# Step 1's first convolution block: three pairs by DMA and three adds on VectorE; two lists reordered; another PSUM bank for the side products

## The chip, the cores and the metric

The kernel runs on one core of one Trainium2 chip. The metric is the time of one execution on the device in microseconds, the median of three runs; lower is better. The core has TensorE (PE, matmuls), VectorE (DVE), ScalarE (ACT), GpSimd (POOL) and SyncE (SP). POOL and SP also issue DMAs, each from a queue of its own, worked off in order.

## The reference, cut to what matters

A causal convolution over the sequence with 7 taps, whose weights are a softmax per head, feeds a two-layer feed-forward block:

```python
w = softmax(weight)                             # 8 heads x 7 taps
out[b, s, h] = sum_k w[h, k] * x_pad[b, s + k, h]  # B=8, S=4096, D=192
x = out.reshape(B * S, D)                       # 32768 tokens
h = x @ w_in                                    # 192 -> 2048
g = h * (1.0 / (1.0 + np.exp(-1.702 * h)))
return g @ w_out                                # 2048 -> 192
```

Everything is in fp32.

## The kernel before, in words

**Tiling.** The tokens are worked off in 32 steps ("big" 0 to 31); each takes 512 tokens of two halves of the batch. A step has a convolution, a first product into the hidden layer (`hidden`, called once for each of two halves `v`, or `plain` in step 0), the gelu, and a second product (`second`, or `second_first` in step 0). Both products are done by schemes in the manner of Strassen: sums of blocks of the operands, fewer products, and sums of their results. Step s + 1's convolution is computed while step s's products run, so that TensorE need not wait.

**The convolution.** A step's input has three blocks of 64 channels, c = 0, 1, 2. Block 1 is computed on DVE (`conv`, L504). For blocks 0 and 2, ACT multiplies the input by each tap into a place of its own (`tap`, L515), and the taps are then added. For step 1 they are added by DMAs that accumulate, issued on POOL (`end_taps`, L529), along a tree (`TREE`): with the places numbered 0 to 6, after tap 2 the pair 1 += 2, after tap 4 the pair 3 += 4, and after tap 6 the pair 5 += 6 and then 0 += 1, 3 += 5 and 0 += 3, the last three each waiting for what they read. For step 2 block 0 goes by the same tree and block 2 by GpSimd adds (L517).

**Sums of blocks.** `prepare` yields a step's work in order: block 1 on DVE, a wait for the taps, eight sums and differences of blocks (`SUMS_C`, L393 and L391; V1 first, for step 1 on DVE), and copies over to the other half of the partitions by DMAs on SP (`cross`, L540): V1 alone, then the four blocks below C31, and after the last sum the remaining eight, C31 to V8. `need(label)` works the list off up to a label: "conv 1" (block 1), "first 1" (V1 and its copy), "all 1" (everything).

**Step 0's second product** (`second_first`) is an order written out by hand. PE runs 42 steps of it; in each, `go` puts three matmuls of 32 output columns side by side and one matmul of a side list (`aside`, L820) into the fourth quarter of a PSUM bank (`sums[0]`, `sums[1]` or `c12`), from where ACT copies finished sums away (L822). DVE makes its operands: t1, t2 (sums of blocks of g, 128x2048 each), s1 to s4 (of w_out), and `sums_b` (L827). At the same time ACT copies and POOL's DMAs build the sums of w_out that later steps use (`add_forms`, stages 0 to 3: COPY_O by ACT, L435 and L433; SUMS_O by accumulating DMAs on POOL, L437; some read what an earlier one made). ACT changes the sign of four of these at the end (`end_forms`, L441). DVE makes 20 sums of blocks of w_in in place (`SUMS_W`, `sums_w_in`). Taps of step 2 are put between (`next_tap`); their places are rows of g.

**What sets the order.** Each engine runs its instructions in program order, and waits for what the next one needs. POOL's queue holds, in this order: the adding DMAs of step 1's taps, block 2 and then block 0; add_forms stages 0, 1 and 2; the DMAs of step 2's block 0; one GpSimd add; add_forms stage 3; further GpSimd adds. SP's queue holds step 1's three copies over, the stores of step 0's output, and the loads of x for step 3.

Step 1's first half begins with `pe(x, 5)`, that is block 0 of w_in with C11, then `pe(sums, 12)`, block 13 with V4, which is among the eight blocks copied last. In the second half the fifth product needs ACT's copy of `sums` (L646), which stands behind `end_forms` in ACT's queue.

Of the kernel before, what the change touches and what calls it, by code (L numbers as in the profile page):

```python
# [15 lines left out]
def kernel(  # L16
# [64 lines left out]
    vec, act = nc.vector, nc.scalar  # L81
# [28 lines left out]
    sums = [psum.tile([P, TOK], F32, name=f"sums{h}") for h in range(2)]  # L110
# [59 lines left out]
    def place(big, b):  # L170

        if b == V1:
            return V8 if big % 2 else C31
        return C31 if b == V8 and big % 2 else b

    def own(big):
        return conv_t[:, big % 2 * 2, :, :]
# [3 lines left out]
    NA = 21  # L181
    w_in_s = consts.tile([P, NA, UW], F32)
    SUMS_W = [
        (12, 10, "n", 11),
        (13, 12, "-", 2),
        (14, 3, "-", 12),
        (12, 1, "-", 13),
        (15, 4, "+", 13),
        (16, 3, "+", 5),
        (17, 2, "+", 5),  # L190
        (18, 0, "+", 3),
        (19, 6, "+", 8),
        (20, 19, "+", 10),
        (4, 4, "n", 16),
        (5, 2, "+", 11),
        (0, 0, "+", 2),
        (10, 7, "-", 10),
        (7, 7, "+", 19),
        (8, 8, "-", 11),
        (11, 9, "+", 11),  # L200
        (11, 11, "-", 19),
        (9, 9, "-", 3),
        (3, 3, "0", 3),
    ]

    TERMS = [
# [12 lines left out]
    def form(i):  # L219

        if i < WHOLE:
            return w_out_s[:, i // NG, i % NG * NG : (i % NG + 1) * NG, :]
        return w_form[:, i - WHOLE, :, :]
# [165 lines left out]
    def add_up(v, dst, a, op, b, eng=vec):  # L389
        if op == "+":  # L390
            eng.tensor_add(v(dst), v(a), v(b))  # L391
        elif op == "-":
            eng.tensor_sub(v(dst), v(a), v(b))  # L393
        elif op == "n":
            vec.scalar_tensor_tensor(
                out=v(dst), in0=v(a), scalar=-1.0, in1=v(b), op0=ALU.mult, op1=ALU.subtract
            )
        else:
            vec.tensor_scalar_mul(v(dst), v(a), -1.0)

    def sums_w_in(i):
        add_up(lambda j: w_in_s[:, j, :], *SUMS_W[i])

# [26 lines left out]
    def add_forms(stage):  # L430
        for dst, src, *sign in COPY_O[stage]:
            if sign:
                act.mul(form(dst), form(src), -1.0)  # L433
            else:
                act.copy(form(dst), form(src))  # L435
        for dst, src in SUMS_O[stage]:
            nc.gpsimd.dma_start(out=form(dst), in_=form(src), accum_op=ALU.add)  # L437
# [49 lines left out]
    def tap_home(big, c, k):  # L487
        if big == 1:
            return homes_1[c][k - 1]
        if big < 3:  # L490
            return (first_taps if c == 0 else taps[3])[k - 1]
        return taps[c][k - 1]

    def conv_src(big, c, k, ns=slice(0, 2)):
        return xts[big][:, c, ns, Q - PAD + k : Q - PAD + k + T]

    def conv(big, c, k, ns=slice(0, 2), times=vec.tensor_scalar_mul):
        src = conv_src(big, c, k, ns)
        dst = own(big)[:, 2 * c + ns.start : 2 * c + ns.stop, :]
        tap = cw[:, c, k : k + 1]  # L500
        if k == 0:
            times(dst, src, tap)
        else:
            vec.scalar_tensor_tensor(  # L504
                out=dst, in0=src, scalar=tap, in1=dst, op0=ALU.mult, op1=ALU.add
            )

    DMA_TAPS = (0,)
    TREE = {2: [(1, 2)], 4: [(3, 4)], 6: [(5, 6), (0, 1), (3, 5), (0, 3)]}

    def tap(big, c, k):

        dst = own(big)[:, 2 * c : 2 * c + 2, :]
        home = tap_home(big, c, k) if k else dst
        act.mul(home, conv_src(big, c, k), cw[:, c, k : k + 1])  # L515
        if k and c not in DMA_TAPS and big > 1:
            nc.gpsimd.tensor_add(dst, dst, home)  # L517
            return
        homes = [dst] + [tap_home(big, c, i) for i in range(1, K)]
        for a, b in TREE.get(k, ()):  # L520
            tree.append((homes[a], homes[b]))
        end_taps(2 if big == 2 and k == K - 1 else 0)

# [2 lines left out]
    def end_taps(left=0):  # L526
        while len(tree) > left:
            out, src = tree.pop(0)
            nc.gpsimd.dma_start(out=out, in_=src, accum_op=ALU.add)  # L529

    def sums_c(big, i):
        add_up(
            lambda j: own(big)[:, place(big, j), :],
            *SUMS_C[i],
            eng=vec if big == 1 else nc.gpsimd,
        )
# [28 lines left out]
    def cross_when(early, *what):  # L565
        if given[early] < what[0] - 1:
            waiting[early].append(what)
        else:
            cross_now(early, *what)
# [7 lines left out]
    def prepare(big):  # L577

        v1 = place(big, V1)
        def convs(*cs):  # L580
            for c in cs:
                for k in range(K):
                    yield "", 0.76 if k else 0.48, lambda c=c, k=k: conv(big, c, k)

        cost = 0.34 if big == 1 else 0.0
        yield from convs(1)
        yield f"conv {big}", 0.0, lambda: None
        yield f"done {big}", 0.0, lambda: need(f"taps {big}")
        yield "", cost, lambda: sums_c(big, 0)
        yield f"first {big}", 0.0, lambda: cross_when(True, big, v1, v1 + 1)  # L590
        yield "", 0.0, lambda: cross_when(False, big, 0, C31)
        for i in range(1, len(SUMS_C)):
            yield "", cost, lambda i=i: sums_c(big, i)
        rest = (C31, V8) if big % 2 else (C31 + 1, NB)
        yield f"all {big}", 0.0, lambda: cross_when(False, big, *rest)
# [159 lines left out]
    def chunk_cols(c):  # L755
        return slice(c * Q, (c + 1) * Q)

    def second_first(between, fetch, last_taps):
# [7 lines left out]
        def place4(t):  # L766
            return t.rearrange("p (v h e) -> p v h e", v=2, h=2)
# [3 lines left out]
        def rows4(n, pi):  # L771
            return pairs[:, :, pi // 2, n, :, pi % 2, :]
# [3 lines left out]
        b11, b12, b21, b22 = ([rows4(n, pi[j]) for pi in groups] for j in range(2) for n in range(2))  # L776
# [4 lines left out]
        t2 = [place4(flat_room[:, t4 : 2 * t4]), place4(osbs)]  # L781
# [10 lines left out]
        add, sub = vec.tensor_add, vec.tensor_sub  # L792
        js = slice(0, TOK // Q)

        c11, a, c12, c21 = (slots[i][h] for h in range(2) for i in range(2))
        side = []

        def listed(w, t, gs=(0, 1)):
            return [
                (w[i][:, v, h, :], t[i][:, v, :, h * T : (h + 1) * T])  # L800
                for i in gs for v in range(2) for h in range(2)
            ]
# [9 lines left out]
        def go(bank, steps, first=True, more=False):  # L812
            for i, (w, t) in enumerate(steps):
                for c in range(NC):
                    nc.tensor.matmul(
                        chunk(bank, c), w[:, chunk_cols(c)], t,
                        start=first and i == 0, stop=not more and i == len(steps) - 1, skip_group_check=True,
                    )
                dst, w, t, start, to = side.pop(0)
                nc.tensor.matmul(dst, w, t, start=start, stop=to is not False, skip_group_check=True)  # L820
                if to is not False:
                    act.copy(to, dst)  # L822
# [3 lines left out]
        def sums_b(i):  # L826
            sub(b12[i], b22[i], b12[i])  # L827
# [8 lines left out]

        p2, p3 = listed(a12, b21), listed(s4, b22)
        aside(
            (sums[0], sums[1], c12),
            (listed(s1, t1, (0,)), None, True), (listed(s1, t1, (1,)), p5, False), (p3[:6], q12, False),  # L840
        )
        last_taps()
# [5 lines left out]
        for i in range(2):  # L848
            sub(s2[i], s1[i], a11[i])
        add_forms(0)  # L850
        need("conv 1")
        for i in range(2):
            sub(s4[i], a12[i], s2[i])
            sub(s3[i], a11[i], a21[i])
        go(c11, p2[:6], more=True)
        add_forms(1)
        sums_b(0)
        sums_b(1)
        go(a, listed(s2, t2), first=False)
        act.copy(whole(c12), whole(a))  # L860
        go(c11, p2[6:], first=False)
        need("first 1")
        sub(t2[0], b21[0], t2[0])
        sub(t2[1], b21[1], t2[1])
        need("all 1")
        add(p1, p1, whole(c11))
        go(a, listed(s3, b12), first=False)
        add_forms(2)
# [4 lines left out]
        fetch()  # L873
        for i in range(len(SUMS_W)):
            sums_w_in(i)
# [22 lines left out]
    def chunk(t, c):  # L898
        return t[c * Q : (c + 1) * Q]
# [155 lines left out]
    def need(label):  # L1055
        for q in (todo, ready):
            while any(item[0] == label for item in q):
                q.pop(0)[2]()
# [179 lines left out]
    def fetch(big, v, slot):  # L1238

        need(f"first {big}")  # L1240
        terms(big, v, slot, 16, first=True)
# [6 lines left out]
    for big in range(1, N_BIG):  # L1248
        more = big + 1 < N_BIG
        last = hidden(big, 0, x, z, y, sums, work, lambda: fetch(big, 1, z))  # L1250
        x, z, y, sums = z, x, sums, y
# [39 lines left out]
```

## Time and profile before

| | |
|---|---|
| median of 3 runs | 2292.73 us (2292.44 to 2292.82) |
| profiled execution, its own time | 2293.8 us |
| its span (first to last instruction) | 2292.1 us |
| PE busy in the span | 2271.0 us (99%) |
| DVE, ACT, POOL busy | 1935.3, 1563.6, 844.4 us |
| granted TensorE clock, mean | 0.996 |

Times within the trace are counted from the start of the span. Of step 0's second product PE runs 55.9 to 94.1 us; step 1's first product begins behind it. A row of a timeline has the start, the duration, engine, line, operation and tiles (out<-in), how many instructions are merged in it, and in brackets the idle time of the engine before it with what ended it. Line numbers are those of the kernel before.

### The profile page before, as it was taken

What the parts mean: (1) busy time and instruction counts of PE and PEld (TensorE: products, weight loads), DVE (VectorE), ACT (ScalarE), POOL (GpSimd) and SP (SyncE); (2) the same over time, 40 slices, a digit from 0 to 9 for tenths busy, and PEclk for the clock granted to TensorE, in tenths of its full rate; (3) what the DMA queues carried; (4) which work ended last, traced back from release to release, by engine and by line L of the source; (5) the groups of instructions that cost most, each with busy time, mean ns of one, the idle gap of its engine ahead of it and who ended that gap; (6) DMA issues with size and microseconds to landing.
All of it is one profiled execution on the core that took longest, in us unless ns stands there. A gap on an engine that the chain in (4) does not pass through costs nothing.

```text
span 2292.1 us, 60960 instructions
## 1 busy us (share of the span) xinstructions
PE 2271.0 (99%) x25214; PEld 1203.4 (53%) x25214; DVE 1935.3 (84%) x2791; ACT 1563.6 (68%) x2968; POOL 844.4 (37%) x837
## 2 busy tenths in 40 slices
PE   9989999999999999999999999999999999999999
PEld 5355555555555555555555555555555555555556
DVE  8778888888888888888888888888888888888877
ACT  8647766677666677666776667776667766677754
POOL 1444433344423434334444234443334442344400
PEclk9989999999999999999999999999999999999999
DMA  9975667565665756666656656566666566564443
GB/s 204 163 143 114 115 125 141 123 130 112 125 136 121 141 111 116 125 139 125 129 113 127 134 121 140 112 114 126 139 126 128 113 127 135 122 139 86 91 98 70
DMA packets 270660, 286.56 MB, mean 125 GB/s; under 512 B 118064, under 2 KB 206128, under 8 KB 270256
## 3 DMA queue, kind: packets, MB, share of 16 engines
q0 software_dynamic: 58080, 151.48, 36.8%
q1 hardware_dynamic: 210656, 130.80, 25.3%
q8 instruction: 199, 3.26, 0.6%
q14 instruction: 77, 0.63, 0.1%
q10 hardware_dynamic: 1648, 0.39, 0.1%
HBM read 53.15 MB, written 25.17 MB: 34 GB/s over the span
## 4 chain that ended last, share of the span: by engine, by line
PE 94%; DMA 4%; DVE 1%; POOL 1%; SPq 0%; issue 0%; ACT 0%; POOLq 0%; ACTq 0%; DVEq 0%
PE slot L609 33%; PE slot L986 33%; PE sums L609 15%; PE sums L986 12%; DMA w_form<-w_form 1%; DMA g<-g 1%; DMA g<-in_moe_w_in_dram 1%; DMA conv_t<-conv_t 0%; POOL w_form L437 0%; SPq L296 0%; DMA osbs<-in_moe_w_out_dram 0%; DMA w_out_s<-w_form 0%; SPq L99 0%; ACT w_form L515 0%; POOL conv_t L529 0%
## 5 line engine op out<-in xcount | busy, mean ns | idle before, releaser
L609 PE MATMUL slot<-conv_t,w_in_s 64*128 64x512 f32 x3740 | 862.3, 593 | 9.8 <-ACT room L646 5.8
L986 PE MATMUL slot<-g,w_form 128*32 128x256 f32 x7024 | 710.3, 379 | 0.0
L609 PEld LDWEIGHTS slot<-conv_t,w_in_s 64*128 64x128 f32 x3740 | 374.8, 188 | 439.6 <-issue 354.3
L393 DVE TENSOR_TENSOR g<-g 128x1024 f32<-128x1024 f32 x372 | 451.2, 1240 | 8.1 <-ACT g L635 4.9
L986 PEld LDWEIGHTS slot<-g,w_form 128*32 128x32 f32 x7024 | 373.5, 110 | 119.7
L609 PE MATMUL sums<-conv_t,w_in_s 64*128 64x512 f32 x1660 | 407.3, 593 | 3.9 <-DMA conv_t<-conv_t 3.7
L635 ACT ACTIVATE g<-room 128x1024 f32<-128x1024 f32 x310 | 325.6, 1077 | 72.2 <-DVE room L650 72.2
L1011 ACT COPY room<-slot 32x256 f32<-32x256 f32 x434 | 159.3, 367 | 310.4 <-PE slot L986 309.3
L986 PE MATMUL sums<-g,w_form 128*32 128x256 f32 x2648 | 368.8, 379 | 0.0
L986 PE MATMUL slot<-g,w_out_s 128*32 128x256 f32 x4080 | 318.8, 380 | 0.0
L962 POOL DMA_DIRECT2D g<-g x124 | 106.4, 858 | 500.0 <-PE sums L986 166.6
L609 PEld LDWEIGHTS sums<-conv_t,w_in_s 64*128 64x128 f32 x1660 | 170.9, 188 | 191.7 <-issue 142.0
L517 POOL TENSOR_TENSOR conv_t<-conv_t,g 128x512 f32<-128x512 f32 x180 | 260.4, 1447 | 15.2 <-POOL conv_t L517 2.7
L529 POOL DMA_DIRECT2D g<-g x120 | 104.3, 884 | 428.1 <-PE sums L986 119.4
L646 ACT COPY room<-slot 128x512 f32<-128x512 f32 x434 | 231.4, 600 | 41.7 <-PE slot L609 41.7
L515 ACT ACTIVATE g<-xt,cw 128x512 f32<-128x512 f32 x360 | 248.4, 729 | 2.2
L986 PEld LDWEIGHTS slot<-g,w_out_s 128*32 128x32 f32 x4080 | 164.7, 110 | 131.7 <-ACT g L631 22.7
L631 ACT ACTIVATE g<-slot 128x512 f32<-128x512 f32 x334 | 180.7, 598 | 45.2 <-PE slot L609 25.1
L986 PEld LDWEIGHTS sums<-g,w_form 128*32 128x32 f32 x2648 | 177.9, 110 | 36.7
L504 DVE SCALAR_TENSOR_TENSOR conv_t<-xt,cw,conv_t 128x512 f32<-128x512 f32 (+1 forms) x198 | 185.6, 938 | 4.6
L393 POOL TENSOR_TENSOR conv_t<-conv_t 128x256 f32<-128x256 f32 x180 | 182.5, 1028 | 9.4
L1011 ACT COPY room<-sums 32x256 f32<-32x256 f32 x217 | 79.6, 367 | 144.7 <-PE sums L986 142.5
(203 smaller groups left out, 2901.8 us busy)
## 6 DMA issues: line engine op xcount, KB each, us to landing
g<-g POOLq DMA_DIRECT2D x124, 512.0 KB, 5.6
xin<-in_x_dram SPq DMA_DIRECT2D x240, 180.0 KB, 4.3
conv_t<-conv_t SPq DMA_DIRECT2D x180, 192.0 KB, 3.2
g<-g POOLq DMA_DIRECT2D x120, 256.0 KB, 3.9
out_dram<-osbs SPq DMA_DIRECT2D x186, 128.0 KB, 5.0
g<-room POOLq DMA_DIRECT2D x31, 512.0 KB, 5.4
conv_t<-g POOLq DMA_DIRECT2D x60, 256.0 KB, 4.6
g<-osbs POOLq DMA_DIRECT2D x30, 512.0 KB, 4.8
```

What stands on the lines that cost most here:

```text
L393: eng.tensor_sub(v(dst), v(a), v(b))
L504: vec.scalar_tensor_tensor(out=dst, in0=src, scalar=tap, in1=dst, op0=ALU.mult, op1=ALU.add)
L515: act.mul(home, conv_src(big, c, k), cw[:, c, k : k + 1])
L517: nc.gpsimd.tensor_add(dst, dst, home)
L529: nc.gpsimd.dma_start(out=out, in_=src, accum_op=ALU.add)
L609: nc.tensor.matmul(slot[h], w_in_s[halves[h], a, v * P : (v + 1) * P], src, start=first, stop=True, skip_group_check=True,)
L631: act.activation(dst[:, :, h, :], src[h].rearrange("p (o t) -> p o t", o=2), AF.Gelu_apprx_sigmoid)
L635: act.activation(dst.rearrange("p o h t -> p h o t"), src.rearrange("p h (o t) -> p h o t", o=2), AF.Gelu_apprx_sigmoid,)
L646: act.copy(bank(dst, h), bank(src, h))
L962: nc.gpsimd.dma_start(out=spot(dst), in_=spot(a), accum_op=ALU.add)
L986: nc.tensor.matmul(dst, w, t, start=first, stop=last, skip_group_check=True)
L1011: act.copy(to, d)
```

## The change

1. The taps of step 1's block 0 are added along a shorter tree, `PAIRS_1`: only the pairs 1 += 2, 3 += 4 and 5 += 6 by DMA. Three adds on DVE (128x512 each) put places 1, 3 and 5 onto place 0; they stand behind block 1 in `prepare(1)`. The three DMAs 0 += 1, 3 += 5 and 0 += 3 are gone.
2. In `second_first`, `need("first 1")` stands where `need("conv 1")` stood, so V1 and its copy come ahead of s3, s4 and `sums_b`; these are taken by halves, and `need("all 1")` comes ahead of the two t2 sums, which change places.
3. The 20 sums of w_in are in another order; each is the same sum.
4. The third bank of the side list is `c11` in place of `c12`.

```diff
     SUMS_W = [
+        (18, 0, "+", 3),
+        (0, 0, "+", 2),
         (12, 10, "n", 11),
         (13, 12, "-", 2),
...
+    PAIRS_1 = {2: [(1, 2)], 4: [(3, 4)], 6: [(5, 6)]}
...
-        for a, b in TREE.get(k, ()):
+        for a, b in (PAIRS_1 if big == 1 and c == 0 else TREE).get(k, ()):
             tree.append((homes[a], homes[b]))
...
         yield f"conv {big}", 0.0, lambda: None
+        if big == 1:
+            dst = own(1)[:, 0:2, :]
+            for k in (1, 3, 5):
+                yield "", 0.7, lambda k=k: vec.tensor_add(dst, dst, tap_home(1, 0, k))
         yield f"done {big}", 0.0, lambda: need(f"taps {big}")
...
         aside(
-            (sums[0], sums[1], c12),
+            (sums[0], sums[1], c11),
...
         add_forms(0)
-        need("conv 1")
+        need("first 1")
+        go(c11, p2[:6], more=True)
+        add_forms(1)
         for i in range(2):
             sub(s4[i], a12[i], s2[i])
             sub(s3[i], a11[i], a21[i])
-        go(c11, p2[:6], more=True)
-        add_forms(1)
-        sums_b(0)
-        sums_b(1)
+            sums_b(i)
         go(a, listed(s2, t2), first=False)
         act.copy(whole(c12), whole(a))
         go(c11, p2[6:], first=False)
-        need("first 1")
+        need("all 1")
+        sub(t2[1], b21[1], t2[1])
         sub(t2[0], b21[0], t2[0])
-        sub(t2[1], b21[1], t2[1])
-        need("all 1")
         add(p1, p1, whole(c11))
```

More of the change, by code (lines that the diff above doesn't have):

```diff
@@ L183 @@
     SUMS_W = [
+        (18, 0, "+", 3),
+        (0, 0, "+", 2),
         (12, 10, "n", 11),
         (13, 12, "-", 2),
-        (14, 3, "-", 12),
-        (12, 1, "-", 13),
-        (15, 4, "+", 13),
         (16, 3, "+", 5),
         (17, 2, "+", 5),
-        (18, 0, "+", 3),
+        (5, 2, "+", 11),
+        (14, 3, "-", 12),
+        (15, 4, "+", 13),
         (19, 6, "+", 8),
[L193 to L198, printed above, removed]
         (8, 8, "-", 11),
         (11, 9, "+", 11),
-        (11, 11, "-", 19),
         (9, 9, "-", 3),
         (3, 3, "0", 3),
+        (20, 19, "+", 10),
+        (12, 1, "-", 13),
+        (4, 4, "n", 16),
+        (10, 7, "-", 10),
+        (11, 11, "-", 19),
+        (7, 7, "+", 19),
     ]
```

## The prediction

> **What bounds the kernel now.** I read the page first, for who is busy, and then who waited for whom on PE, over the whole span.
>
> ```profile
> PE 2271.0 (99%) x25214; PEld 1203.4 (53%) x25214; DVE 1935.3 (84%) x2791; ACT 1563.6 (68%) x2968; POOL 844.4 (37%) x837
> ```
> ```profile
> PE slot L609 <- ACT room L646: 5.8, 1, 5.8
> PE slot L609 <- ACT g L631: 3.7, 1, 3.7
> PE sums L609 <- DMA conv_t<-conv_t: 3.7, 1, 3.7
> ```
>
> PE is busy nearly throughout. The reader is to see that each of these three waits happens once, and that they make 13.2 us; the other PE waits are below 1.5 us each and stand in the first 20 us. So a change in this stretch can only be worth what these waits cost. Where they stand, PE's timeline shows:
>
> ```profile
> 75.66 0.62 PE L820 MATMUL slot<-w_in_s,conv_t 128*32 128x512 f32 x1
> ...
> 76.55 0.61 PE L815 MATMUL slot<-g,conv_t 128*32 128x512 f32 x3
> ...
> 85.13 1.02 PE L820 MATMUL sums<-g,conv_t 128*32 128x512 f32 x2
> ...
> 94.14 1.13 PE L609 MATMUL slot<-conv_t,w_in_s 64*128 64x512 f32 x4
> 98.93 2.08 PE L609 MATMUL sums<-conv_t,w_in_s 64*128 64x512 f32 x4 [3.66 <-DMA conv_t<-conv_t]
> ...
> 116.03 1.90 PE L609 MATMUL sums<-conv_t,w_in_s 64*128 64x512 f32 x8
> 121.67 5.88 PE L609 MATMUL slot<-conv_t,w_in_s 64*128 64x512 f32 x16 [3.74 <-ACT g L631]
> 133.36 2.56 PE L609 MATMUL slot<-conv_t,w_in_s 64*128 64x512 f32 x4 [5.80 <-ACT room L646]
> ...
> 138.64 1.78 PE L609 MATMUL slot<-conv_t,w_in_s 64*128 64x512 f32 x4
> ```
>
> A matmul takes about 0.215 us of the row at full speed (116.03: eight in 1.90, of which 0.18 is the overlap at the end). Behind each wait they are slower. From 98.93 to the end of the 116.03 row there are 80, 17.2 us at full speed, and they took 19.0: 1.8 lost. The 16 of 121.67 took 5.88 in place of 3.4: 2.4 lost. The 16 from 133.36 to 140.42 took 7.06 in place of 3.4: 3.6 lost. Waits and slow restarts together are 13.2 + 7.8 = 21.0 us; the most that can be had.
>
> Why PE waits, ACT and POOL show, each in its own timeline:
>
> ```profile
> 92.11 1.94 ACT L515 ACTIVATE g<-xt,cw 128x512 f32<-128x512 f32 x3
> ...
> 120.08 1.06 ACT L635 ACTIVATE g<-room 128x1024 f32<-128x1024 f32 x1 [5.91 <-DVE room L650]
> ...
> 123.94 1.35 ACT L441 ACTIVATE w_form<-w_form 128x384 f32<-128x384 f32 x3
> 132.31 0.52 ACT L441 ACTIVATE w_form<-w_form 128x384 f32<-128x384 f32 x1 [7.01 <-DMA w_out_s<-w_form]
> 132.74 1.05 ACT L646 COPY room<-slot 128x512 f32<-128x512 f32 x2
> ```
> ```profile
> 62.27 2.97 POOL L529 DMA_DIRECT2D conv_t<-conv_t  x3
> ...
> 69.72 0.86 POOL L529 DMA_DIRECT2D conv_t<-conv_t  x1 [1.99 <-DMA conv_t<-conv_t]
> 74.00 0.86 POOL L529 DMA_DIRECT2D conv_t<-conv_t  x1 [3.42 <-DMA conv_t<-conv_t]
> 74.54 5.62 POOL L437 DMA_DIRECT2D w_form<-w_out_s  x6
> ...
> 80.93 5.42 POOL L437 DMA_DIRECT2D w_form<-w_out_s  x5
> ...
> 103.16 0.86 POOL L437 DMA_DIRECT2D w_form<-w_form  x1 [11.75 <-DMA w_form<-w_form]
> ...
> 105.96 3.64 POOL L529 DMA_DIRECT2D g<-g  x3
> 112.47 1.19 POOL L529 DMA_DIRECT2D conv_t<-g  x1 [2.88 <-DMA g<-g]
> 117.29 1.19 POOL L529 DMA_DIRECT2D g<-g  x1 [3.62 <-DMA g<-g]
> 123.21 1.19 POOL L529 DMA_DIRECT2D conv_t<-g  x1 [4.74 <-PE slot L609]
> ...
> 126.33 2.90 POOL L437 DMA_DIRECT2D w_out_s<-w_form  x2
> ```
>
> The **third wait** is ACT's: its copy at 132.74 stands behind the last sign change (L441), which waited for the last DMA of add_forms stage 3. That DMA is the end of POOL's queue: tap DMAs of step 1 to 74.00, forms from 74.54, a wait of 11.75 us for a form to land, step 2's tap DMAs from 105.96 in a chain of landings, then stage 3 at 126.33. The **second wait** belongs to the same queue: the gelu at 120.08 writes the rows of g that the tap DMA of 112.47 reads, so it waits for that DMA, though the profile names DVE. The **first** is the copy over of the last eight blocks. So POOL's queue is what sets the end of this stretch, and PE waits for it.
>
> **The change part by part.** *The three tree DMAs go.* POOL is done with the pairs at 62.27 + 2.97 = 65.2 and starts the forms there, not at 74.54: 9.3 us sooner. ACT's copies that the forms add to are made in the same order as before. Can the DMA engines take it? The windows say how full they are (the last two columns are their share and GB/s):
>
> ```profile
> 70.00:75.00 5.00, 5.00 (x51) 1.55 (x46) 2.87 (x2) 1.03 (x2) 1.58 (x3) 1.00 0.38 67
> 75.00:100.00 25.00, 21.34 (x172) 6.17 (x168) 21.93 (x42) 11.71 (x20) 13.09 (x15) 0.97 1.07 189
> ```
>
> They are full from 75 to 100 us and at 0.38 from 70 to 75. The full stretch holds a fixed amount of work (forms, three copies over); begun 9.3 us sooner and without idle time, it ends up to 9.3 sooner. The bounds are 0 (the copies over do not come sooner and forms only queue) and 9.3; I take 9.3, since the gap it fills is there. POOL's waiting form goes from 103.16 to 93.9, step 2's tap DMAs from 105.96 to 96.7; their last ACT taps are done at 94.05 (92.11 and 1.94).
>
> From there the chain is one of landings (median us from issue to landing in the last column; x3 are the taps of 105.96, x1 that of 117.29, w_out_s the last forms):
>
> ```profile
> conv_t<-conv_t POOLq DMA_DIRECT2D x3, 256.0 KB, 5.3
> ...
> g<-g POOLq DMA_DIRECT2D x3, 256.0 KB, 8.1
> ...
> g<-g POOLq DMA_DIRECT2D x1, 256.0 KB, 5.4
> ...
> w_out_s<-w_form POOLq DMA_DIRECT2D x2, 192.0 KB, 5.1
> ```
>
> Step 1's three pairs, of the same size and nearly alone, took 5.3 in place of 8.1, and the single DMA of 74.00 landed within 3.4 (DVE's row below) in place of 5.4. Before, the loads of x ran beside step 2's; they follow the stores, which follow DVE's last sums and hardly move, so now they fall more onto the end of the chain. This is worth between 0 and 2.8 + 2.0 = 4.8; I take 2.7, the middle. So stage 3 lands 9.3 + 2.7 = **12.0 us sooner**, and PE's third restart moves from 133.36 to 121.4.
>
> *DVE: three adds, and a new wait.* The rows that carry DVE:
>
> ```profile
> 63.48 3.11 DVE L504 SCALAR_TENSOR_TENSOR conv_t<-xt,cw,conv_t 128x512 f32<-128x512 f32 x4
> ...
> 77.37 0.42 DVE L393 TENSOR_TENSOR conv_t<-conv_t 128x256 f32<-128x256 f32 x1 [4.49 <-DMA conv_t<-conv_t]
> ...
> 84.90 0.68 DVE L866 TENSOR_TENSOR conv_t<-conv_t,slot 96x512 f32<-96x512 f32 x1
> ...
> 95.30 0.29 DVE L399 TENSOR_SCALAR w_in_s<-w_in_s 128x256 f32<-128x256 f32 x1
> ```
>
> An add of 512 columns has its nearest row at 84.90: 0.68 each, 2.0 in all. The last pair had landed at 69.72 (POOL's row), so the third add ends at 70.4 and V1 at 70.8 rather than 77.8. Queued behind this wait are s3, s4 and both `sums_b`, which PE needs from the row of 76.55 on: DVE's block between 66.6 and 72.9 (77.37 less 4.49), 6.3 us. It now runs 70.8 to 77.1, its first half done at 74, 2.5 us ahead of PE; the second half is needed half of a product later, some 3.4 us. Hidden; if the pairs landed over 2.5 us later, PE would pay the excess. The other seven sums (2.8 us, to 84.90 before) end at 80 rather than 84.9, so the eight blocks are sent 4.9 us sooner, against a wait of 3.66: the first wait goes, with 1 to 2 us to spare. The t2 sums end at 84.6, and PE takes them behind the row of 85.13 and one product more, from 86 on. All DVE work behind ends within 0.5 us of before: the new adds fill the wait of 4.49 that goes.
>
> *Order of w_in.* Block 0 is wanted first by PE (at 94.14) and was 13th of 20; all 20 were done at 95.6 (the row of 95.30). PE comes 0.9 us earlier now and does not stop behind 94.14, so the old order could cost it up to about 1.5 us with sums wanted before 95.6; with the new one, in the order in which PE wants them, nothing.
>
> *The bank.* At 75.66 a side matmul waited for ACT's copy into the same bank; the side list then ran one step late, and its last two matmuls stood alone at 85.13. With c11 that goes: 0.9 us of PE.
>
> *PE alone.* It reaches the second half at 117.93 - 0.9 - 3.7 - 1.8 + 1.0 = 112.5. The 1.0 is for new short waits (the z bank is freed by DVE, and ACT's first copy comes late); bounds 0 and 2. The gelu of 120.08 made PE wait 3.74, so at 116.3 it would have done no harm; PE being 5.4 us ahead, it now must come by 110.9. The tap DMA that it waits for lands 9.3 to 12.0 sooner, at 108 to 110.8: the second wait goes, barely. PE stands before its fifth product at 112.5 + 3.4 = 115.9 and must wait for ACT until 121.4: the third wait remains at 5.5, and with it a slow restart like the one before.
>
> **The sum.** Third restart 12.0 sooner, nothing lost or gained behind it: 2293.8 - 12.0 = 2281.8 for an execution like the profiled one, whose own time is 1.1 above the median. By the median of 2292.73 it is **2280.7**. All the PE gains (7 us) go into the last wait.
>
> The Trainium skill, "TensorE: Matmul & The Clock Gate" (What's actually happening), has the clock halve after an idle window of about 3.4 us. By that page a remaining wait well under this would save the slow restart as well; the trace agrees as far as it goes, since its three slow restarts follow waits of 3.66 and more.
>
> **The rivals.** *A: POOL's chain ends in time and all three waits go.* Then PE alone counts: 21.0 + 0.9 - 1.0 = 20.9, which is 2271.8. It needs the last sign change 17.5 us sooner (121.4 less 115.9, beside the 12.0); even the most that I found, 9.3 + 4.8 = 14.1, falls short. A shorter wait with part of the restart saved lies between, 2272 to 2276.
>
> *B: the forms only queue.* If the DMA engines, not POOL's queue, set when forms land, stage 3 lands as before, and whatever PE gains is waited for at 133.36: 2292.7, no change. For it: the share of 1.07 for 25 us. Against: the share of 0.38 just ahead, and three DMAs of 256 KB fewer.
>
> *C: slower.* POOL's 15 form issues now stand beside DVE work throughout. One issue under a busy DVE took long:
>
> ```profile
> 78.93 2.11 POOL L437 DMA_DIRECT2D w_form<-w_form  x1
> ```
>
> At 2.11 each against 0.94 (74.54: six in 5.62) POOL would lose 15 x 1.17 = 17.6 us and stage 3 come 5.6 us later than before: 2298.3. It is slower than before from 1.74 us an issue. Against it: five in 5.42 at 80.93, with DVE busy too, are 1.08 each. The Trainium skill speaks for this rival: "DMA: Bandwidth & Descriptors" (SWDGE vs HWDGE vs iDMA) says that GpSimd writes its DMAs' descriptor rings into SBUF, where VectorE can lock it out in some of its modes.
>
> **How the numbers follow.** A measurement of this kernel can tell about 0.2% (4.6 us) from no change. Forecast, 7 to 16 us sooner: 0.62. A and what lies towards it: 0.17. Between 4.6 and 7 sooner (DMA order eats part): 0.05. B, within 4.6: 0.10. C: 0.06. Faster 0.62 + 0.17 + 0.05 = 0.84, same 0.10, slower 0.06. The range leaves out B, C and the weakest gains: from A's 2271.5 to 2285.5 (7.2 sooner).
>
> **What would show it.** Right: L437 on POOL begins near 65, V1 near 70.5, no wait of PE for a copy over, L820 never alone at 85, the tap DMAs of step 2 near 97, PE's only long wait for ACT's L646 ending near 121, and it is the last sign change that holds ACT. Wrong: forms that begin at 65 but land no sooner (B), issues of 2 us (C), or a PE wait near 76 for DVE.

## The result, and the profile after

| | before | after |
|---|---|---|
| median of 6 runs each, side by side | 2292.93 us (2292.44 to 2293.97) | 2285.00 us (2283.56 to 2286.97) |
| ratio after/before, 95% interval | | 0.9965 [0.9952, 0.9978] |
| profiled execution, its own time | 2293.8 us | 2284.85 us |
| its span | 2292.1 us | 2282.9 us |

The changed kernel is 0.35% faster: 7.9 us by the medians, 8.95 between the two profiled executions. Forecast were 12.0. Lines behind L507 have other numbers now: L609 of before is L614, L646 is L651, L820 is L825, L529 is L530.

Who is busy (the page of after), and the whole span's waits of PE over 1 us (total, times, longest):

```profile
PE 2266.0 (99%) x25214; PEld 1202.3 (53%) x25214; DVE 1934.6 (85%) x2794; ACT 1563.2 (68%) x2968; POOL 847.4 (37%) x834
```
```profile
PE slot L614 <- ACT room L651: 8.6, 1, 8.6
PE sums L455 <- POOL osbs masks.py:199: 1.4, 1, 1.4
PE slot L1076 <- ACT g L1068: 1.1, 1, 1.1
```

Of the three waits in this stretch one is left, and it has grown from 5.8 to 8.6 us. PE's timeline of after shows where:

```profile
93.07 1.13 PE L614 MATMUL slot<-conv_t,w_in_s 64*128 64x512 f32 x4
94.03 1.02 PE L614 MATMUL sums<-conv_t,w_in_s 64*128 64x512 f32 x4
...
112.53 3.76 PE L614 MATMUL slot<-conv_t,w_in_s 64*128 64x512 f32 x15
124.93 2.56 PE L614 MATMUL slot<-conv_t,w_in_s 64*128 64x512 f32 x4 [8.64 <-ACT room L651]
```

At 94.03, where PE had stood 3.66 us for the last eight blocks, it goes straight on. The second half begins at 112.53 without a wait for the gelu; before, PE was ready for it at 117.93 and began at 121.67. PE stands before its fifth product at 116.29, 11.3 us ahead of before's 127.56, and goes on at 124.93, only 8.4 us ahead of 133.36. The first and second waits went. Of PE's lead of 11.3 us, 2.8 are spent in a longer third wait.

What it waits for, on ACT and POOL of after:

```profile
110.40 1.06 ACT L640 ACTIVATE g<-room 128x1024 f32<-128x1024 f32 x1 [1.78 <-DMA conv_t<-g]
...
114.26 1.35 ACT L441 ACTIVATE w_form<-w_form 128x384 f32<-128x384 f32 x3
123.88 0.52 ACT L441 ACTIVATE w_form<-w_form 128x384 f32<-128x384 f32 x1 [8.26 <-DMA w_out_s<-w_form]
124.31 1.05 ACT L651 COPY room<-slot 128x512 f32<-128x512 f32 x2
```
```profile
61.70 2.97 POOL L530 DMA_DIRECT2D conv_t<-conv_t  x3
64.09 5.88 POOL L437 DMA_DIRECT2D w_form<-w_out_s  x6
...
94.07 0.86 POOL L437 DMA_DIRECT2D w_form<-w_form  x1 [12.48 <-DMA w_form<-w_form]
...
95.62 3.98 POOL L530 DMA_DIRECT2D g<-g  x3
101.66 1.19 POOL L530 DMA_DIRECT2D conv_t<-g  x1 [2.06 <-PE sums L614]
107.28 1.19 POOL L530 DMA_DIRECT2D g<-g  x1 [4.43 <-DMA g<-g]
114.78 1.19 POOL L530 DMA_DIRECT2D conv_t<-g  x1 [6.32 <-PE slot L614]
...
117.89 2.90 POOL L437 DMA_DIRECT2D w_out_s<-w_form  x2
```

It is the same chain as before, begun sooner. Set against the rows of before, each step shows how much of the lead is left: POOL's waiting form 9.1 us (94.07 for 103.16), step 2's first tap DMA 10.3 (95.62 for 105.96), the fourth 10.8 (101.66 for 112.47), the fifth 10.0 (107.28 for 117.29), the sixth 8.4 (114.78 for 123.21), stage 3 8.4, the last sign change 8.4 (123.88 for 132.31). So at the first tap DMA the lead is 1.0 us more than forecast (10.3 for 9.3), and 2.4 us of it are lost between the fourth and the sixth. The brackets put the waits of these two down to PE, but both read what earlier tap DMAs write: the rows of before put the fourth's wait (2.88 us) down to such a landing, g<-g, and in the kernel with late sign changes below the profile does so with the sixth's (6.41 us).

### The profile page after: what moved, and what is told of

It reads as the page before. It is cut to its first block, busy times and chain, and to the rows that moved or that the text cites. A ratio compares the mean times of both kernels' runs of the same rounds, so it can differ in the third digit from the quotient of the medians.

```text
span 2282.9 us, 60959 instructions
## 1 busy us (share of the span) xinstructions
PE 2266.0 (99%) x25214; PEld 1202.3 (53%) x25214; DVE 1934.6 (85%) x2794; ACT 1563.2 (68%) x2968; POOL 847.4 (37%) x834
## 4 chain that ended last, share of the span: by engine, by line
PE 94%; DVE 2%; DMA 2%; ACT 1%; issue 0%; POOL 0%; SPq 0%; DVEq 0%; POOLq 0%; ACTq 0%
PE slot L614 33%; PE slot L989 33%; PE sums L614 15%; PE sums L989 12%; DMA g<-g 1%; DMA w_form<-w_form 0%; DMA conv_t<-conv_t 0%; DVE xt L473 0%; DMA w_out_s<-w_form 0%; DVE g L832 0%; DVE conv_t L504 0%; DVE w_in_s L391 0%; DMA xin<-in_x_dram 0%; DVE w_in_s L393 0%; DVE w_out_s L376 0%
## 5 line engine op out<-in xcount | busy, mean ns | idle before, releaser
L614 PE MATMUL slot<-conv_t,w_in_s 64*128 64x512 f32 x3740 | 862.1, 592 | 8.9 <-ACT room L651 8.6
L614 PEld LDWEIGHTS slot<-conv_t,w_in_s 64*128 64x128 f32 x3740 | 374.8, 187 | 435.7 <-issue 352.4
L614 PE MATMUL sums<-conv_t,w_in_s 64*128 64x512 f32 x1660 | 408.5, 591 | 0.3 <-DVE w_in_s L376 0.3
L614 PEld LDWEIGHTS sums<-conv_t,w_in_s 64*128 64x128 f32 x1660 | 172.0, 187 | 187.8 <-issue 142.6
L530 POOL DMA_DIRECT2D g<-g x120 | 104.7, 890 | 424.4 <-PE sums L989 128.7
L651 ACT COPY room<-slot 128x512 f32<-128x512 f32 x434 | 231.5, 601 | 41.4 <-PE slot L614 41.4
```

The source lines that it names most:

```text
L614: nc.tensor.matmul(slot[h], w_in_s[halves[h], a, v * P : (v + 1) * P], src, start=first, stop=True, skip_group_check=True,)
L651: act.copy(bank(dst, h), bank(src, h))
```

## The experiments

The theory at the start: the whole gain is the three tree DMAs taken out of POOL's queue (part 1); parts 2 to 4 help PE only, and what they give goes into the wait for POOL's last form. The rival: reordering and bank give a share of their own, or the wait is not POOL's queue but ACT's place in it.

### Part 1 alone, and all but part 1

Before plus part 1, nothing else:

```diff
+    PAIRS_1 = {2: [(1, 2)], 4: [(3, 4)], 6: [(5, 6)]}
...
-        for a, b in TREE.get(k, ()):
+        for a, b in (PAIRS_1 if big == 1 and c == 0 else TREE).get(k, ()):
...
+        if big == 1:
+            dst = own(1)[:, 0:2, :]
+            for k in (1, 3, 5):
+                yield "", 0.7, lambda k=k: vec.tensor_add(dst, dst, tap_home(1, 0, k))
```

> The kernel before with part 1 of the change alone (three pairs by DMA, three adds on VectorE); the order of s3, s4, sums_b and t2, the order of w_in and the bank stay as before. Theory (POOL's queue sets the end of the stretch): POOL starts the forms near 65 us as in the changed kernel, the last form of stage 3 lands near 124, and the whole gain is there: 2285 us (2283 to 2288). The eight blocks are copied over later than in the changed kernel (sent near 83), so a short PE wait of 1 to 3 us near 95 may remain, which the third wait swallows. Rival (the reordering on VectorE is what gains): V1 is only 2 us sooner than before and the time stays above 2289.

Measured: 2286.2 us (2282.88 to 2289.46), ratio 0.9970 [0.9958, 0.9981]; span 2283.0. PE's waits in its timeline:

```profile
98.17 1.18 PE L614 MATMUL sums<-conv_t,w_in_s 64*128 64x512 f32 x3 [0.62 <-ACT room L651]
125.27 2.56 PE L614 MATMUL slot<-conv_t,w_in_s 64*128 64x512 f32 x4 [8.32 <-ACT room L651]
```

PE goes on at 125.27, within 0.4 us of the full change. The reverse, the changed kernel with the old tree and without the three adds:

```diff
-    PAIRS_1 = {2: [(1, 2)], 4: [(3, 4)], 6: [(5, 6)]}
...
-        for a, b in (PAIRS_1 if big == 1 and c == 0 else TREE).get(k, ()):
+        for a, b in TREE.get(k, ()):
...
-        if big == 1:
-            dst = own(1)[:, 0:2, :]
-            for k in (1, 3, 5):
-                yield "", 0.7, lambda k=k: vec.tensor_add(dst, dst, tap_home(1, 0, k))
```

> The changed kernel without part 1: the full tree of DMAs, no adds on VectorE; the new order of V1, s3, s4, sums_b, t2, of w_in and the bank stay. Theory: V1 waits on VectorE for the last tree DMA at 77, s3 and sums_b behind it come at 78 to 84, PE waits 3 to 5 us near 76 to 80, POOL's queue is as before and stage 3 lands near 132, so PE's last restart is near 133 and the time that of the kernel before: 2292 to 2295 us. Rival (the reordering gains by itself): 2289 or less.

Measured: 2294.45 us (2291.45 to 2296.37), ratio 1.0006 [0.9997, 1.0014]: no gain. Its DVE and PE timelines:

```profile
77.06 0.43 DVE L393 TENSOR_TENSOR conv_t<-conv_t 128x256 f32<-128x256 f32 x1 [10.71 <-DMA conv_t<-conv_t]
```
```profile
80.77 1.08 PE L815 MATMUL slot<-g,conv_t 128*32 128x512 f32 x3 [4.30 <-DVE g L827]
...
121.60 4.30 PE L609 MATMUL slot<-conv_t,w_in_s 64*128 64x512 f32 x16 [1.66 <-ACT g L631]
134.88 2.56 PE L609 MATMUL slot<-conv_t,w_in_s 64*128 64x512 f32 x4 [8.99 <-ACT room L646]
```

Here V1 waits for the old, later landing, and `sums_b` stands queued behind it on DVE: PE pays 4.30 us at 80.77. That is the price that the prediction put on late pairs (what exceeds 2.5 us): V1 is 7.1 us later than in after (69.94 below), and 7.1 - 2.5 = 4.6. Without part 1, part 2 adds a wait. So the gain is part 1's, as the theory had it: part 1 alone and the whole change (2286.2 and 2285.00 us) are not apart by more than the runs scatter, and parts 2 to 4 alone give nothing.

### The place of ACT's sign changes

The list of pending work is taken up piece by piece, each piece when its cost fits; what is left is done ahead of the second product. One number, the cost given to the four sign changes, leaves them to that point, so that ACT's copy no longer stands behind them. On the changed kernel:

```diff
-            todo.append(("forms", 0.0, end_forms))
+            todo.append(("forms", 50.0, end_forms))
```

> The changed kernel with one number more changed: the four sign changes at the end of the forms (L441 on ScalarE) are taken just ahead of step 1's second product, where they are needed, not ahead of ScalarE's first copy of the second half. Theory (PE's one long wait of 8.6 us is for that copy, queued behind the last sign change, which waits for the last form): the wait at 116 to 125 goes, with its slow restart; next is V1 of step 2, whose copy lands near 131 and is wanted near 128, so some 3 us remain there: 2278 us (2275 to 2281). Rival (PE would have to wait there in any case, for rows of g or for POOL's sums): 2284 or more.

Measured: 2279.75 us (2276.35 to 2283.32), ratio 0.9941 [0.9927, 0.9954]. The wait of 8.6 is gone; another took part of its place:

```profile
132.56 5.61 PE L614 MATMUL slot<-conv_t,w_in_s 64*128 64x512 f32 x12 [3.54 <-DMA conv_t<-conv_t]
```

That is PE waiting for the copy over of step 2's V1. POOL makes V1 behind stage 3 and five adds, so this wait is for work further down the same queue. As expected, the copy was set free. The same number on the kernel before:

> The kernel before with the same one number changed (sign changes ahead of the second product). Theory: its third wait (5.8 us) and the slow restart behind it (3.6 us) go, the first two stay: 2284 us (2282 to 2287), about as much as the whole change. Rival: the time stays at 2291 or more because another wait for POOL's queue takes its place.

Measured: 2288.13 us (2287.25 to 2290.21), ratio 0.9979 [0.9971, 0.9988], 4.8 us faster where 6 to 11 were expected. The third wait went, as it should; the other two stayed (3.96 and 3.81), and step 2's V1 came as a new one:

```profile
142.34 2.94 PE L609 MATMUL slot<-conv_t,w_in_s 64*128 64x512 f32 x12 [1.61 <-DMA conv_t<-conv_t]
```

The expectation's theory had missed this wait; its rival had named one of this kind, but with a time of 2291 or more. Both kernels show that the third wait was ACT standing behind the last sign change, and that POOL's queue is still late further down.

### Step 2's taps in pairs too

If POOL's chain of landings is what is left, it should go away when, in the changed kernel, step 2's block 0 also takes pairs, with GpSimd adding them behind stage 3:

```diff
-        for a, b in (PAIRS_1 if big == 1 and c == 0 else TREE).get(k, ()):
+        for a, b in (PAIRS_1 if big < 3 and c == 0 else TREE).get(k, ()):
...
-        end_taps(2 if big == 2 and k == K - 1 else 0)
+        end_taps()
...
+        for k in (1, 3, 5):
+            nc.gpsimd.tensor_add(own(2)[:, 0:2, :], own(2)[:, 0:2, :], tap_home(2, 0, k))
```

> The changed kernel, and step 2's block 0 of taps treated likewise: three pairs by DMA, then three adds of places 1, 3 and 5, here on GpSimd and behind add_forms stage 3 in POOL's queue. Theory (POOL's chain of landings ahead of stage 3 sets PE's last wait): stage 3 is issued near 101 to 105 us and lands by 112, the last sign change no longer waits, V1 of step 2 is there before 128, and no wait of PE over 1 us remains behind 20 us. Then PE alone counts, as the prediction's first rival worked out: 2272 us (2270 to 2274.5). Rival (another wait follows at once, for instance the gelu that writes rows of g, or V1 of step 2): 2276 or more.

Measured: **2273.69 us** (2273.03 to 2275.70), ratio 0.9918 [0.9904, 0.9931]. POOL and ACT of this kernel:

```profile
95.90 3.98 POOL L530 DMA_DIRECT2D g<-g  x3
...
99.31 4.02 POOL L437 DMA_DIRECT2D w_form<-w_out_s  x2
100.46 4.64 POOL L437 DMA_DIRECT2D w_out_s<-w_form  x2
```
```profile
113.61 1.76 ACT L441 ACTIVATE w_form<-w_form 128x384 f32<-128x384 f32 x4
```

Stage 3 is issued at 100.46 rather than 117.89, and all four sign changes run at 113.61 without a wait. The stretch from 90 to 140 us, in after and then here (first numbers: length, PE busy; last three: granted clock, DMA share, GB/s):

```profile
90.00:140.00 50.00, 41.36 (x189) 25.76 (x183) 32.26 (x53) 34.54 (x61) 28.66 (x26) 0.90 0.72 119
```
```profile
90.00:140.00 50.00, 49.94 (x364) 30.25 (x360) 46.95 (x65) 41.15 (x74) 32.40 (x28) 1.00 0.86 156
```

PE is busy without a gap and the clock is never lowered. Of the 11.5 us between the two spans (2282.9 and 2271.4), 8.64 are the wait, and 2.9 are left, about what the slow restart costs (5.6 us at half clock behind 124.93, by the rows further down, are 2.8 us of work). This is PE alone, the prediction's rival A, reached by another road. It beats both kernels.

Two parts that cost or gave nothing in after were tried here, where PE is the bound. First the side list's bank back:

```diff
-            (sums[0], sums[1], c11),
+            (sums[0], sums[1], c12),
```

> The kernel with step 2's block 0 in pairs too, with the side list's third bank back at c12. Theory (PE alone counts there, and the bank costs PE 0.9 us): a side matmul waits for ScalarE's copy near 75, the last two side matmuls stand alone near 85, and the time is 0.9 us above that kernel's (0.4 to 1.5). Rival (the lag is made up elsewhere): no difference within 0.4.

Measured: 2274.79 us (2273.95 to 2275.13), 1.1 more; the last two side matmuls stand alone again:

```profile
85.00 1.02 PE L825 MATMUL sums<-g,conv_t 128*32 128x512 f32 x2
85.96 1.13 PE L614 MATMUL slot<-conv_t,w_in_s 64*128 64x512 f32 x4
```

The product behind them starts at 85.96, 0.9 us later than the 85.05 without; at the start of step 1's second product the difference is 0.6 (131.81 and 131.18). By the medians alone it would not be clear, since the runs' ranges overlap. Next the old order of `SUMS_W` (block 0 as 13th again, the other 19 back in their places too):

```diff
     SUMS_W = [
-        (18, 0, "+", 3),
-        (0, 0, "+", 2),
         (12, 10, "n", 11),
...
+        (0, 0, "+", 2),
         (10, 7, "-", 10),
```

> The kernel with step 2's pairs too, in which PE waits nowhere behind the start, with the block sums of w_in back in the old order (block 0 as 13th of 20). Theory: PE wants block 0 at 93.1 and all 20 were done by about 95.6 before, so PE waits 0 to 1.5 us for VectorE near 93 to 96 and the time is 0 to 1.5 us above that kernel's 2273.7. Rival: the order decides more, since a wait of PE brings a slow restart too: 2 to 4 us longer, with a granted clock below 1 behind 95.

Measured: 2273.55 us (2273.00 to 2274.03): no difference, and PE waits nowhere near 93 to 96. Part 3 is worth nothing, even here. And the late sign changes (the same number, 0.0 to 50.0, as above):

> The kernel with step 2's pairs too, with the four sign changes put just ahead of the second product as well. Theory (the sign changes no longer hold ACT, since the last form has landed before 113.6): no change, 2273 to 2274.5, PE waits nowhere over 1.5 us. Rival (the late place of the sign changes gives or takes time by itself, as four ACT instructions beside the step's end): 1 to 3 us either way, with a PE wait for ACT or for w_form behind 135.

Measured: 2274.47 us (2273.68 to 2274.93), ratio 0.9915 [0.9900, 0.9929] to before: within 0.8 us of the kernel without, whose ratio is 0.9918 [0.9904, 0.9931]. With the landings early, their place does not matter.

### What stretched the chain

The prediction let the chain get 2.7 us shorter; it got longer. Two things run beside step 2's tap DMAs, both on SP: the six stores of step 0's output (L917) and the eight loads of step 3's x (L99). SP's timeline of after, then of before:

```profile
96.89 6.68 SPq L917 DMA_DIRECT2D out_dram<-osbs  x6
103.61 8.81 SPq L99 DMA_DIRECT2D xin<-in_x_dram  x8
```
```profile
98.03 7.31 SPq L914 DMA_DIRECT2D out_dram<-osbs  x6
105.39 10.88 SPq L99 DMA_DIRECT2D xin<-in_x_dram  x8
```

Before, all stores were issued by 105.34, ahead of the first tap DMA at 105.96; only the last ones' landings and the loads ran beside the taps. After, the tap DMAs start at 95.62 and the stores come only 1.1 us sooner: now both run beside them. First the loads were left out (the kernel does not bring step 3's input):

```diff
-        load_x(3)
```

> The changed kernel without the eight loads of x for step 3, so that step 3 works on the x of step 2 (work left out). Theory (the loads beside step 2's tap DMAs are what made the chain of landings longer than predicted): the first three tap DMAs of step 2 land in some 5 to 6 us, the next two in 4 to 5 each, stage 3 lands near 117 to 119 in place of 123.8, and the time falls by 4 to 7 us, to 2278 to 2281. Rival (they wait for one another, and for stores): landings as before within 1 us, 2283.5 or more.

Measured: 2284.32 us (2282.44 to 2285.49). My theory, that it was the loads, fell: the chain hardly got shorter. Then the stores were left out (step 0's output is not written), the loads being back:

```diff
-        store(0, 0)
...
-        store(0, 1)
```

> The changed kernel without the six stores of step 0's output (work left out: that output is not written). The loads of x for step 3 then follow the copies over directly and come some 10 us sooner, beside the forms. Theory (loads are the disturbance, stores are not): landings of step 2's tap DMAs mixed, since the loads now fall onto the first three: stage 3 lands within 3 us of 123.8, time 2282 to 2286. Rival (the stores, with their many small packets, are what stretched the first landings): stage 3 lands 4 us sooner or more, 2281 or less.

Measured: 2282.66 us (2282.45 to 2283.66). That is inside what was expected, and the last sign change comes 2.0 us sooner than in after. Neither alone accounts for the stretch, so both were left out together:

> The changed kernel with neither the six stores of step 0's output nor the eight loads of step 3's x (the kernel leaves both out). Taken alone, the loads' absence brought the last sign change 1.0 us sooner, the stores' absence 2.0. Theory (in the changed kernel the six tap DMAs of step 2 are stretched by whichever of the two runs beside them): with neither, the first three land within about 4, 5.3 and 6.7 us as step 1's did, and the last three within 3.8 each, so the last form lands at 117 to 119 and PE goes on at 118.5 to 120.5, 4.4 to 6.4 sooner; 2278.5 to 2281. Rival 1 (the stretch is the six DMAs' own, each waiting on the one before, and on forms still in flight): last form lands at 121 or later, PE goes on at 122.5 or later, 2282 to 2285. Rival 2 (POOL's issue or PE's own order holds the chain): landings are short, but idle time of POOL ahead of an issue is put down to something other than a landing.

Measured: 2280.02 us (2277.45 to 2280.48), ratio 0.9936 [0.9919, 0.9952] where after has 0.9965: the theory that both stretch it held, in the landing, in PE's restart and in the time. The last sign change, which starts as the last form lands, in no loads, no stores, neither:

```profile
122.91 0.52 ACT L441 ACTIVATE w_form<-w_form 128x384 f32<-128x384 f32 x1 [7.24 <-DMA w_out_s<-w_form]
```
```profile
121.89 0.52 ACT L441 ACTIVATE w_form<-w_form 128x384 f32<-128x384 f32 x1 [6.92 <-DMA w_out_s<-w_form]
```
```profile
118.75 0.52 ACT L441 ACTIVATE w_form<-w_form 128x384 f32<-128x384 f32 x1 [4.24 <-DMA w_out_s<-w_form]
```

The chain's length is this start less that of step 2's first tap DMA, which in the same order is:

```profile
95.44 3.99 POOL L530 DMA_DIRECT2D g<-g  x3
```
```profile
97.90 4.03 POOL L530 DMA_DIRECT2D g<-g  x3
```
```profile
96.36 3.98 POOL L530 DMA_DIRECT2D g<-g  x3
```

| kernel | first tap DMA | last sign change | chain | PE goes on |
|---|---|---|---|---|
| before (loads and the end of the stores) | 105.96 | 132.31 | 26.35 | 133.36 |
| after (stores and loads) | 95.62 | 123.88 | 28.26 | 124.93 |
| after, no loads (stores beside it) | 95.44 | 122.91 | 27.47 | 123.96 |
| after, no stores (loads issued ahead of it) | 97.90 | 121.89 | 23.99 | 122.94 |
| after, neither | 96.36 | 118.75 | 22.39 | 119.80 |

With neither, the chain is 5.9 us shorter than in after. The stores alone account for 5.1 of it (27.47 - 22.39, no loads in either kernel); the loads, put behind the stores, add 0.8 (28.26 - 27.47). What the loads alone would do to the chain is not shown, because without the stores SP issues them sooner:

```profile
86.74 9.38 SPq L99 DMA_DIRECT2D xin<-in_x_dram  x8
```

All were issued by 96.12, ahead of the first tap DMA at 97.90. They fell on the form ahead of the chain, which starts 2.3 us later, and only their last landings on the tap DMAs (23.99 - 22.39 = 1.6). The kernel before, with the loads beside its chain and the last stores landing as it starts, is 4.0 us above neither. One more kernel bears the stores out: the changed kernel without part 1 has the old tree as before has, but DVE and PE are late there from 80 us on, and with them its stores, which SP issues from 104.00 to 110.71, beside the tap DMAs, which start at 104.64. Its chain takes 29.20 us (to 133.84), where before's takes 26.35. The landings say the same (KB each, median us to landing between 92 and 128 us; g<-g are four of the tap DMAs, conv_t<-g the other two), in after and with neither:

```profile
g<-g POOLq DMA_DIRECT2D x4, 256.0 KB, 7.5
out_dram<-osbs SPq DMA_DIRECT2D x6, 128.0 KB, 8.3
conv_t<-g POOLq DMA_DIRECT2D x2, 256.0 KB, 6.8
```
```profile
g<-g POOLq DMA_DIRECT2D x4, 256.0 KB, 5.1
conv_t<-g POOLq DMA_DIRECT2D x2, 256.0 KB, 5.2
```

The stores themselves land in 8.3 us; before, issued ahead of the taps, they took 4.5.

## Why the prediction was right in kind and 4 us off in size

**What bounds the kernel: right.** The end of POOL's queue set the last wait before and sets it after; moving ACT's sign changes away from it (2279.75), or emptying the chain (2273.69), takes the wait away.

**The forms 9.3 us sooner: right, a little low.** L437 begins at 64.09 for 65.2 forecast, the waiting form is 9.1 sooner. The tap DMAs are 10.3 sooner, 1.0 more. So rival B (the forms only queue) did not happen: the gap in the DMA engines' share was real, and was filled (70 to 75 us: 0.38 before, 1.13 after).

**The chain 2.7 us shorter: this step failed.** "This is worth between 0 and 2.8 + 2.0 = 4.8; I take 2.7, the middle." (The middle is 2.4; the slip is of no weight.) It measured -1.9: 26.35 became 28.26. The bounds came from step 1's pairs "nearly alone", and that size was good (with nothing beside it the chain is 4.0 shorter than before's, 22.39). What failed was the step ahead of it: I followed the loads of x onto the end of the chain, said that the stores hardly move, and did not ask what the tap DMAs move onto when they come 10 us sooner and the stores stay. They moved onto the stores. So a lower bound of 0 had no ground either. In sum 10.3 - 1.9 = 8.4 at PE's third restart for 12.0. Two errors met here: the taps came 1.0 us sooner than forecast, and the chain took 4.6 us longer (2.7 + 1.9). That 2285.00 still lies within the range, 0.5 us from its upper end of 2285.5, is in part luck; two of the six runs lie above it.

**From the restart to the end.** "Nothing lost or gained behind it": 8.4 at the restart are 9.2 in span. Part of that is a shorter slow restart: the half clock ran on for 6.2 us behind 133.36 before, for 5.6 behind 124.93 after (rows below). The runs' medians show 7.9, and after's runs spread over 3.4 us where before's spread over 1.5, so the last us is not to be read closely.

**DVE: right, its end a little sooner.**

```profile
67.69 0.69 DVE L592 TENSOR_TENSOR conv_t<-conv_t 128x512 f32<-128x512 f32 x1 [0.73 <-DMA conv_t<-conv_t]
69.21 0.69 DVE L592 TENSOR_TENSOR conv_t<-conv_t 128x512 f32<-128x512 f32 x1 [0.83 <-DMA conv_t<-conv_t]
69.94 0.42 DVE L393 TENSOR_TENSOR conv_t<-conv_t 128x256 f32<-128x256 f32 x1
...
74.36 2.29 DVE L832 TENSOR_TENSOR g<-g 128x2048 f32<-128x2048 f32 x1
```

The adds took 0.69 for 0.68, V1 is done at 70.36 for 70.8 forecast, and `sums_b` is done at 76.65, in time: PE did not wait near 76. DVE's last turns of step 0's output, forecast within 0.5 us of before, end 1.1 us sooner (97.45 for 98.59), and the stores behind them come 1.1 sooner too.

**PE alone: right.** Second half at 112.53 for 112.5; the second wait "goes, barely": the gelu ran at 110.40, wanted by 110.9. The bank's 0.9 us at the next product is measured (85.96 and 85.05). The order of w_in was given up to about 1.5 us and is worth none.

**The third wait: right that it remains, too small.** 5.5 forecast, 8.64 measured: PE came 0.4 us later than forecast (116.29 for 115.9) and ACT's copy let it go 3.5 later (124.93 for 121.4); the 3.1 between are the chain's late landings.

**Rival C (slow issues under a busy DVE): refuted.** Six form issues took 5.88 us at 64.09, 0.98 each for the 2.11 of that rival, and three took 2.97 at 72.59, in a stretch (70 to 75 us) in which DVE was busy for 5.00 of 5.00 us. What made the one issue of 2.11 us slow in the kernel before stays open. The Trainium skill's "DMA: Bandwidth & Descriptors" (SWDGE vs HWDGE vs iDMA) has VectorE lock GpSimd out of SBUF in some modes; these adds of two fp32 tensors do not show it.

## What to carry to other kernels

When a bound engine waits, go back through the in-order queues to the transfer that lands last, and ask of a fix what stands next in that queue: here each wait that went brought the next one nearer, and only when the whole chain was short did PE run through. When a chain of transfers is moved, list what it will run beside at the new time, what stays put as well as what moves; the neighbours set its length (22.4 us alone, 28.3 beside stores and loads). A saving on the bound engine's own work is worth nothing as long as that engine waits behind it, and close to its full size once it doesn't (the bank: 0.9 us at the next product).

## What the runs showed of the hardware

**Stores beside it lengthen a chain of SBUF-to-SBUF DMAs.** With six stores of 128 KB beside it the chain took 27.47 us, with nothing beside it 22.39; eight loads of 180 KB behind the stores made it 28.26. Whether stores do more than loads in the same place is not shown, and why they lengthen it was not tried.

**The clock is lowered in pieces of about 3.4 us, and a wait does not tell how many.** Windows cut at the steps of the granted clock (the clock is the third number from the end): before's second and third restart, after's, and that of the kernel with neither stores nor loads.

```profile
122.60:126.00 3.40, 3.40 (x10) 1.85 (x9) 1.91 (x1) 2.69 (x5) 2.79 (x4) 0.50 0.35 51
...
129.40:139.60 10.20, 6.24 (x15) 5.10 (x17) 3.86 (x4) 4.51 (x8) 9.65 (x8) 0.50 0.28 47
```
```profile
120.30:130.50 10.20, 5.57 (x13) 4.61 (x15) 3.86 (x4) 4.50 (x8) 9.73 (x8) 0.50 0.34 57
```
```profile
119.20:126.00 6.80, 6.20 (x15) 5.04 (x17) 5.10 (x4) 4.04 (x8) 6.42 (x5) 0.50 0.00 0
```

A wait of 3.74 us brought 3.4 us at half clock, one of 3.72 brought 6.8, and waits of 5.80 and 8.64 brought the same 10.2. The Trainium skill's "TensorE: Matmul & The Clock Gate" (What's actually happening) says that the window is free-running, so that it does not start with the wait; the steps here agree with that, being multiples of 3.4 us at places of their own. In all four the clock comes back at the end of the first piece in which PE ran throughout: from 122.6 to 126.0 behind the restarts at 121.67 and 119.80, from 136.2 to 139.6 behind 133.36, from 127.1 to 130.5 behind 124.93. So behind these restarts the half clock cost from 1.7 us (3.4 at half speed) to 3.1 (6.2 at half speed), an estimate from these rows. The clock can also go down early: at 129.4 PE had stood for only 1.8 us (from 127.56). So a wait well under 3.4 us does not surely keep the clock up, as the prediction had it by the Trainium skill; waits of 1.61 us (late sign changes in the kernel before) and 1.66 us (the changed kernel without part 1) did.

**The runs' scatter differs between kernels, and the cause stays open.** The ranges are 3.4 us (after), 6.6 (part 1 alone) and 7.0 (late sign changes) against 1.0 to 2.7 for the four kernels with step 2's pairs. A long wait of PE does not explain it: the kernel before, with three waits, has 1.5, and the one without the stores, with a wait of 6.50 us, has 1.2.
